# A three-part fp32 kernel: the first products of its recurrence into idle tiles, input loads moved, masks as steps of their own, and the state copied by DMA

## The chip, the cores and the metric

The kernel runs on one core of a Trainium2 chip. The metric is the device time of one execution in microseconds (us). A profile of one execution lists the instructions of each engine: PE (TensorE, matrix products; PEld is its weight load), DVE (VectorE), ACT (ScalarE), POOL (GpSimd) and SP (SyncE, which here only issues DMAs).

## What is computed

Batch 4, 8 heads, 768 time steps, head size 40, all fp32. First a recurrence on a 40 x 40 state for each batch and head, then a channel mix (a low-rank mix over time, two dense layers with relu), then an attention with 4 experts of which the 2 best are summed. Cut to what matters:

```python
for t in range(768):                      # the recurrence
    y[:, :, t] = einsum('bhd,bhde->bhe', r_t, state)
    Sa = einsum('bhde,bhe->bhd', state, a_t)
    state = state * w_t[:, :, None, :] - einsum('bhd,bhe->bhde', Sa, b_t) + einsum('bhd,bhe->bhde', v_t, k_t)
x = y.transpose(0, 2, 1, 3).reshape(4, 768, 320)
u = x + (x.T @ U @ V).T                   # the channel mix
x = u + relu(u @ w_ch1) @ w_ch2
# then causal softmax attention for each of 4 experts, weighted sum of the best 2
```

## The kernel before, in words

The recurrence is worked in chunks of 64 time steps: 12 chunks (`NC`) for 2 pairs of batches (`NBP`), 24 units (`NU`) in all. A unit holds 8 pairs of heads (`PP`). The change lies in `recurrence`; the channel mix and the attention behind it stay as they are.

For each unit there are three kinds of work:

- **Front.** `scaled(j)` makes running products of the decay on DVE (the scans of L195 and L203, tile `P`), scales two inputs into the tile `bkt` (L208) and a third in place (L216), and SP copies that one into the zeroed tile `ga` (L219). There are 16 sets (`NSET`) for 24 units: rows 40 to 63 and 104 to 127 of a set hold a third, "guest" unit's data, which `sent(j)` copies by DMA to the guest tiles `P_g` and `bkt_g` and to the guest's `ga` (L164). The sets are loaded into four slots at first (`ldt` twice and the unused part of `x` twice), later into two. `front(u)` then transposes on PE (L233, L243), and multiplies `bkt` with `ga` (L255); ACT copies this product `pg` from PSUM back over `bkt` (L258); POOL takes from it the diagonal blocks for the solve (`lx`, L263), masks it into `ga` (L266) and keeps a corner (`m21`, L270).
- **Solve.** For each group of 4 units `lanes(g)` inverts the triangular blocks on DVE: a transpose (L279), 30 steps of a product (L285) and a sum (L288), a transpose back into `tf` (L297). There are 6 groups.
- **Core and output.** `core(u)` needs `tf`, `ga`, `m21` and the state, works on PE and ACT in turns, and adds to the state `st` (L362, L364 on DVE; L367 puts it into the tile `uv` of the next unit). `outs(u)` transposes the tile `xu` (L381), which holds the unit's values and the state, multiplies (L403), masks (L396, DVE) and writes the unit's output (L416, L420, L426). The state gets into `xu` by `carry`: two POOL copies for each of 22 units (L306).

The order of all this is written out by hand in `ORDER_R`, a string with one letter for each step of a generator: `d` scaled, `g` sent, `f` fronts, `m` loads, `l` one step of a solve, `A` and `B` the cores of the two batch pairs, `p` and `q` their outputs, `z` the zeroing of tiles, `y` first loads, `u` the conversion of weights for the channel mix (L542 to L550), `x` a product for it. `WAIT` gives how many letters the masking, the output product and the state update are put off behind the PE work that they read. Each engine runs its instructions in the order in which the letters issue them, and SP issues its DMAs in that order too; each waits for what it reads and for the buffers that it writes.

The tiles `rbd` and `uvt` belong to the outputs and are not used before the first output.

Of the kernel before, what the change touches and what calls it, by code (L numbers as in the profile page):

```python
# [39 lines left out]

WAIT = (2, 3, 3)
ORDER_R = (
    'zddlllllldllllmgdlmgdlzfdldlglfmfgfzdgfdmfllyfgmlfffmfdfdfmmddllfflglmlgdffddgdglgllffldzl',
    'ffglldllllmlllfzylflllldflllflylfffldllflgldflflglffldlggylllfllgdmBffllAfflflflfffgAldlll',
    'BlmdlllfdfBgABAfqBAllfqlqBAddlgllldgmpdpldBlgllAqpgllfBAlffBAqfqqfpBAppflgllldddllffBmlffl',
    'qplfllqfqldpdlglflAlqffflBAgqplBdAgBlAfpqBpAplmlldldlfgdllgpqqBllllAflfglplAlBpfplAlBllAfl',
    'llfqBpfAmBqgqpdAlflldqlldlllllflffplqqgBlddfflllpplglfmlAdBggfdqllfpBABAflpllqBllplqlfddll',
    'glflqlfdfplBlfflmdpgqABfpfqlqldfABpABpplAllgfAqgBldqmAlfpdfdlplglffgBgllfplfddlfqllpffAfdl',  # L50
    'lgfqlqlAfllflllmlllBlAfABppABpgqfBqlqAddppfgllAllBlqdqllpdfggBlqlqldffAlBgAlBfpAqlpqBlffll',
    'ffflfllpflflfllpulpqAlBplAqlqBAllulqBllAlpqBpAxBlqlllxlllAlppqllxxlBAlllqulpBAqlqlBlABplpl',
    'AllppBxqllllqlllllAqlllpBplqqlABullplqBAllBAlpqplquBAllpqlpxxllluBApqpBlAqqlBAlluBAlqqppAq',
    'qpxlllullxxqppqllpqulplqlBplllxxllx',
)


def recurrence(ctx, tc, ld, vin, rv, ident, xs, keep, wpool, mix):
# [29 lines left out]
    tfs = [const.tile([128, 32, 32], F32, name=f"tf{i}") for i in range(2)]  # L88

    ldx = [x[:, NC // 3:].rearrange("p c f -> p (c f)")[:, :LDW] for x in xs]  # L90
    guests = [fpool.tile([128, PP, CW], F32, name="P_g"), fpool.tile([128, PP, 2, C], F32, name="bkt_g")]
    nc.gpsimd.memset(guests[0], 1.0)
    nc.gpsimd.memset(guests[1], 0.0)

    def slot(j):
        return (ldt + ldx)[j % 4 if j < 6 else j % 2]

    mix.spare = lambda: fpool.tile([128, 2 * (S // 4)], F32, tag="lx", name="spare")
    BK, GA, PC, LX, M21, TF, UP = {}, {}, {}, {}, {}, {}, {}

    def load_ld(j, a=0, b=LDW):
        nc.sync.dma_start(slot(j)[:, a:b], ld[j, :, a:b])

    def load_v(u):
        c, bp = divmod(u, NBP)
# [117 lines left out]
    def front(u):  # L223

        g, uu = divmod(u, GU)
        c, bp = divmod(u, NBP)
        P, early = PF[u], u < GU
        pc = PC[u] = const.tile([128, PP], F32, tag="pc", bufs=16, name=f"pc{u}")
        nc.scalar.activation(pc, P[:, :, C], AF.Copy)
        pt = ps.tile([128, 4, 2, D], F32, tag="f", bufs=3, name=f"pt{u}")  # L230
        for p in range(4):
            for b in range(2):
                nc.tensor.matmul(pt[64 * b:64 * b + 64, p], P[:, 2 * p + b, :C],  # L233
                                 ident.rearrange("p (r e) -> p r e", r=2)[:, :, :D], start=True, stop=True)
        nc.scalar.activation(xs[bp][:, c], pt.rearrange("p a r d -> p (a r d)"), AF.Copy)
        yield

        bkt = BKT[u]
        BK[u] = wpool.tile([128, PP, 2, D], F32, tag="bk", bufs=AHEAD + 4, name=f"bk{u}")
        for h in range(2):  # L240
            pb = ps.tile([128, HP, 128], F32, tag="f", bufs=3, name=f"pb{u}_{h}")
            for p in range(HP):
                nc.tensor.transpose(pb[:, p], bkt[:, h * HP + p].rearrange("p k t -> p (k t)"), ident)  # L243
            nc.scalar.activation(BK[u][:, h * HP:h * HP + HP],
                                                 pb.rearrange("p q (r e) -> p q r e", r=2)[:, :, :, :D], AF.Copy)
            yield

        ga = GA[u]
        m21 = M21[u] = const.tile([128, PP, 32], F32, tag="m21", bufs=AHEAD + 1, name=f"m21{u}")
        if uu == 0:  # L250
            LX[g] = fpool.tile([128, 32, 32], F32, tag="lx", name=f"lx{g}")
        for h in range(2):
            pg = ps.tile([128, HP, 2, C], F32, tag="o" if early else "f", bufs=3, name=f"pg{u}_{h}")
            for p in range(HP):
                nc.tensor.matmul(pg[:, p], bkt[:, h * HP + p].rearrange("p k t -> p (k t)"),  # L255
                                 ga[:, :, h * HP + p], start=True, stop=True)
            hs = slice(h * HP, h * HP + HP)
            nc.scalar.activation(bkt[:, hs], pg, AF.Copy)  # L258
            if h:
                for r in range(2):  # L260
                    for i in range(2):
                        q = slice(64 * r + 32 * i, 64 * r + 32 * i + 32)
                        nc.gpsimd.tensor_copy(LX[g][q, uu * PP:uu * PP + PP], bkt[q, :, r, 32 * i:32 * i + 32])  # L263
                for r in range(2):
                    z = slice(64 - 64 * r, 128 - 64 * r)
                    nc.gpsimd.affine_select(ga[z, r], bkt[z, :, r], [[0, PP], [1, C]], OP.is_gt, 0.0, base=0,  # L266
                                            channel_multiplier=-1)
                for r in range(2):
                    q = slice(64 * r, 64 * r + 32)
                    nc.gpsimd.tensor_copy(m21[q], bkt[q, :, r, 32:])  # L270
# [208 lines left out]
    for x in "".join(ORDER_R):
# [570 lines left out]
```

## Time and profile before

| | |
|---|---|
| median of 3 runs | 858.09 us (856.68 to 860.68) |
| the profiled execution | 858.54 us, of which the span of instructions is 856.8 |
| PE, DVE busy in the span | 780.3 us (91%), 579.5 us (68%) |
| ACT, POOL busy | 469.9 us (55%), 323.9 us (38%) |
| DMA packets, bytes | 53201, 61.47 MB |
| last solve ends (L297) | 324.0 us |

The span is counted from the first instruction. A busy share over the whole span is an average over stages with different limits, so the stages are looked at apart. A wait is put down to what came last. Durations on POOL are rough.

### The profile page before, as it was taken

What the parts mean: (1) busy time and instruction counts of PE and PEld (TensorE: products, weight loads), DVE (VectorE), ACT (ScalarE), POOL (GpSimd) and SP (SyncE); (2) the same over time, 40 slices, a digit from 0 to 9 for tenths busy, and PEclk for the clock granted to TensorE, in tenths of its full rate; (3) what the DMA queues carried; (4) which work ended last, traced back from release to release, by engine and by line L of the source; (5) the groups of instructions that cost most, each with busy time, mean ns of one, the idle gap of its engine ahead of it and who ended that gap; (6) DMA issues with size and microseconds to landing.
All of it is one profiled execution on the core that took longest, in us unless ns stands there. A gap on an engine that the chain in (4) does not pass through costs nothing.

```text
span 856.8 us, 22703 instructions
## 1 busy us (share of the span) xinstructions
PE 780.3 (91%) x9100; PEld 666.2 (78%) x9100; DVE 579.5 (68%) x1388; ACT 469.9 (55%) x1125; POOL 323.9 (38%) x456
## 2 busy tenths in 40 slices
PE   5666989989999897989899999999999999999997
PEld 4555888988898687877678888887778788887875
DVE  6599999988998997448624131322268868778773
ACT  3534867766677678723323231312168757767672
POOL 5664464536545324315513220202027344244430
PEclk9787999998999999899999999999999999999999
DMA  5554256555545364512100100000000010000101
GB/s 166 171 143 158 78 171 164 151 144 150 137 144 145 87 171 114 130 54 83 47 1 25 34 2 1 1 1 0 1 1 2 1 47 2 16 32 2 47 2 47
DMA packets 53201, 61.47 MB, mean 72 GB/s; under 512 B 31208, under 2 KB 38376, under 8 KB 51560
## 3 DMA queue, kind: packets, MB, share of 16 engines
q1 hardware_dynamic: 53096, 60.02, 24.6%
q8 instruction: 72, 1.18, 0.6%
q14 instruction: 33, 0.27, 0.1%
HBM read 47.46 MB, written 4.13 MB: 60 GB/s over the span
## 4 chain that ended last, share of the span: by engine, by line
PE 54%; DVE 19%; DMA 6%; issue 5%; ACT 4%; POOL 2%; SPq 1%; DVEq 0%; POOLq 0%; ACTq 0%
PE po L943 4%; PE ph L743 3%; PE pa L760 3%; PE ph L740 3%; PE pa L761 3%; PE pa L762 3%; PE ph L741 3%; PE ph L739 3%; PE tp L930 3%; DVE lt L288 3%; DVE tmp L285 3%; PE pn L403 2%; PE pw L343 2%; PE ps L890 2%; PE ps L889 2%
## 5 line engine op out<-in xcount | busy, mean ns | idle before, releaser
L913 POOL TENSOR_TENSOR P<-P,sm 128x128 f32<-128x128 f32 (+2 forms) x92 | 82.9, 931 | 127.6 <-DVE sm L903 115.4
L747 DVE SCALAR_TENSOR_TENSOR hl<-ph,hh 128x512 fp32r<-128x512 f32 x60 | 41.1, 690 | 118.6 <-ACT hh L746 116.1
L746 ACT ACTIVATE hh<-ph 128x512 fp32r<-128x512 f32 x60 | 35.1, 594 | 108.5 <-PE pa L762 101.2
L894 ACT ACTIVATE P<-ps,mx 128x640 f32<-128x640 f32 (+4 forms) x96 | 60.5, 634 | 26.1 <-DVE mx L892 18.1
L285 DVE TENSOR_TENSOR tmp<-lt 128x30 f32<-128x30 f32 (+9 forms) x180 | 70.3, 390 | 3.9
L288 DVE TENSOR_TENSOR lt<-lt,tmp 128x30 f32<-128x30 f32 (+9 forms) x180 | 69.0, 384 | 3.7
L892 DVE CUSTOM_DVE_ANT_0 ps<-ps,neg 128x640 f32<-128x640 f32 (+4 forms) x96 | 59.0, 639 | 7.6 <-PE ps L890 6.5
L263 POOL COPY lx<-bkt 32x256 f32<-32x256 f32 x64 | 30.0, 469 | 87.9 <-ACT bkt L258 85.8
L403 PE MATMUL pn<-rbd,uvt 128*128 128x128 f32 x384 | 54.9, 293 | 7.3 <-DMA uvt<-in_rin 5.7
L776 POOL TENSOR_TENSOR t<-t,ul 128x512 f32<-128x512 f32 x12 | 15.4, 1294 | 116.8 <-DVE t L775 116.7
L255 PE MATMUL pg<-ga,bkt 128*128 128x128 f32 x256 | 40.1, 318 | 19.6 <-DMA ga<-ldt 14.3
L403 PEld LDWEIGHTS pn<-rbd,uvt 128*128 128x128 f32 x384 | 49.6, 204 | 9.5 <-issue 4.9
L930 PE MATMUL tp<-ident,P 128*128 128x128 f32 x336 | 52.0, 276 | 1.8 <-ACT pt L934 0.8
L255 PEld LDWEIGHTS pg<-ga,bkt 128*128 128x128 f32 x256 | 36.6, 226 | 21.6 <-issue 12.7
L346 ACT ACTIVATE uv<-pw 32x320 f32<-32x320 f32 x96 | 41.1, 428 | 18.4 <-PE pw L343 16.7
L739 PE MATMUL ph<-uh,w 128*128 128x512 f32 x120 | 47.1, 399 | 1.7 <-ACT uh L728 1.6
L740 PE MATMUL ph<-ul,w 128*128 128x512 f32 x120 | 47.7, 397 | 0.6 <-DVE ul L729 0.6
L741 PE MATMUL ph<-uh,w 128*128 128x512 f32 x120 | 47.3, 396 | 0.0
L761 PE MATMUL pa<-hl,w 128*128 128x512 f32 x120 | 47.1, 392 | 0.0
L930 PEld LDWEIGHTS tp<-ident,P 128*128 128x128 f32 x336 | 39.4, 140 | 9.2 <-POOL P L913 2.7
L943 PE MATMUL po<-pt,vals 128*64 128x256 f32 (+3 forms) x320 | 45.1, 397 | 1.4 <-DVE o L959 1.0
L762 PE MATMUL pa<-hh,w 128*128 128x512 f32 x120 | 46.2, 391 | 0.0
(217 smaller groups left out, 2239.8 us busy)
## 6 DMA issues: line engine op xcount, KB each, us to landing
ldt<-in_ld SPq DMA_DIRECT2D x12, 1028.5 KB
uvt<-in_rin SPq DMA_DIRECT2D x48, 128.0 KB
rpt<-in_rin SPq DMA_DIRECT2D x24, 256.0 KB
rbd<-in_rin SPq DMA_DIRECT2D x48, 96.0 KB
uv<-in_vin SPq DMA_DIRECT2D x48, 80.0 KB
out<-o SPq DMA_DIRECT2D x24, 160.0 KB
ga<-ldt SPq DMA_DIRECT2D x28, 80.0 KB
room<-in_w SPq DMA_DIRECT2D x7, 320.0 KB
```

The costliest lines, as they stand in the source:

```text
L255: nc.tensor.matmul(pg[:, p], bkt[:, h * HP + p].rearrange("p k t -> p (k t)"), ga[:, :, h * HP + p], start=True, stop=True)
L285: nc.vector.tensor_tensor(tv, L[:, s + 1:, s:s + 1].to_broadcast([128, n, s]), L[:, s:s + 1, :s].to_broadcast([128, n, s]), op=OP.mult)
L288: nc.vector.tensor_tensor(L[:, s + 1:, :s], L[:, s + 1:, :s], tv, op=OP.add)
L403: nc.tensor.matmul(pn[h][:, p], ut[:, h * HP + p].rearrange("p r t -> p (r t)"), rbd[u % 2][:, :, h * HP + p], start=True, stop=True)
L739: nc.tensor.matmul(ph, w[:, 0, f], uh[:, ft], start=ft == 0, stop=False)
L740: nc.tensor.matmul(ph, w[:, 0, f], ul[:, ft], start=False, stop=False)
L741: nc.tensor.matmul(ph, w[:, 1, f], uh[:, ft], start=False, stop=False)
L761: nc.tensor.matmul(pa[ft], w[:, o:o + m], hl, start=False, stop=False)
L762: nc.tensor.matmul(pa[ft], w[:, 2 * DM - FT[2][0] + o:2 * DM - FT[2][0] + o + m], hh, start=False, stop=last)
L913: nc.gpsimd.tensor_tensor(p, p, sm[:, i:i + 1].to_broadcast([128, w]), op=OP.mult)
L930: nc.tensor.transpose(pt[:, j - j0], P[:, c:c + 128], ident)
L943: nc.tensor.matmul(po[64 * r:64 * r + 64, s0:w], VS[b][:, j, HD * e:HD * e + HD], PT[r][:, j, s0:], start=j == 0, stop=j == i1 - 1, skip_g ...
```

## The change

- The first four units' products `pg` are copied to `rbd` and `uvt` (the list `rooms`) instead of back over `bkt`; POOL reads them there.
- The masks (L266, L270) become a generator of their own, `kept(u)`, letter `k`, and can stand later than the copies for the solve.
- Set 1 is loaded complete in front of everything; set 2 is loaded by two DMAs that ACT issues; the loads from set 3 on are one DMA each, and the new order puts them ahead of DMAs of guests.
- `carry` copies the state into `xu` with two DMAs on SP instead of two POOL copies.
- `WAIT` and `ORDER_R` are new (the ten strings are not shown in full).

```diff
-WAIT = (2, 3, 3)
+WAIT = (1, 0, 2)
 ORDER_R = (
-    'zddlllllldllllmgdlmgdlzfdldlglfmfgfzdgfdmfllyfgmlfffmfdfdfmmddllfflglmlgdffddgdglgllffldzl',
+    'dddglzddlfzzfglgglldffldfdlmfddkfylgglldzdflmfldfdffffkdlgllllldfkfgdflmllfdflffdglgllzlfl',
...
+    rooms = [t.rearrange("p r q t -> p (r q t)").rearrange("p (q r t) -> p q r t", q=PP, r=2) for t in rbd] + uvt
...
-    def load_ld(j, a=0, b=LDW):
-        nc.sync.dma_start(slot(j)[:, a:b], ld[j, :, a:b])
+    def load_ld(j, a=0, b=LDW, queue=nc.sync):
+        queue.dma_start(slot(j)[:, a:b], ld[j, :, a:b])
...
     def loads():
-        for j in range(1, NSET):
-            for y in parts[j == 1:] if j < 4 else ((0, LDW),):
-                load_ld(j, *y)
-                yield
+        for j in range(3, NSET):
+            load_ld(j)
+            yield
...
-            nc.scalar.activation(bkt[:, hs], pg, AF.Copy)
+            gm = GM[u] = rooms[u] if early else bkt
+            nc.scalar.activation(gm[:, hs], pg, AF.Copy)
             if h:
                 for r in range(2):
                     for i in range(2):
...
-                        nc.gpsimd.tensor_copy(LX[g][q, uu * PP:uu * PP + PP], bkt[q, :, r, 32 * i:32 * i + 32])
-                for r in range(2):
-                    z = slice(64 - 64 * r, 128 - 64 * r)
-                    nc.gpsimd.affine_select(ga[z, r], bkt[z, :, r], [[0, PP], [1, C]], OP.is_gt, 0.0, base=0,
-                                            channel_multiplier=-1)
-                for r in range(2):
-                    q = slice(64 * r, 64 * r + 32)
-                    nc.gpsimd.tensor_copy(m21[q], bkt[q, :, r, 32:])
+                        nc.gpsimd.tensor_copy(LX[g][q, uu * PP:uu * PP + PP], gm[q, :, r, 32 * i:32 * i + 32])
...
+    def kept(u):
+        ga, gm = GA[u], GM[u]
+        m21 = M21[u] = const.tile([128, PP, 32], F32, tag="m21", bufs=AHEAD + 1, name=f"m21{u}")
+        for r in range(2):
+            z = slice(64 - 64 * r, 128 - 64 * r)
+            nc.gpsimd.affine_select(ga[z, r], gm[z, :, r], [[0, PP], [1, C]], OP.is_gt, 0.0, base=0,
+                                    channel_multiplier=-1)
+        for r in range(2):
+            q = slice(64 * r, 64 * r + 32)
+            nc.gpsimd.tensor_copy(m21[q], gm[q, :, r, 32:])
+        yield
...
     def carry(u):
-                nc.gpsimd.tensor_copy(xu[u % NBP][q, :, r, :D], st[u % NBP][q])
+                nc.sync.dma_start(xu[u % NBP][q, :, r, :D], st[u % NBP][q])
...
     parts = (n, LDW), (0, 2 * PP * C), (2 * PP * C, n)
-    for a, b in parts:
-        load_ld(0, a, b)
-    load_ld(1, *parts[0])
+    for j in range(2):
+        for a, b in parts:
+            load_ld(j, a, b)
...
+    for a, b in (parts[0], (0, n)):
+        load_ld(2, a, b, nc.scalar)
```

**SP at the start.** These are SP's issues before the change, from the 14th on (`x` holds the sets 2 and 3, `ldt` the sets 0, 1, 4, 5; set 2 is `x_66`, set 3 `x_67`):

```order
L102 DMA x_66<-in_ld 128x521
L164 DMA P_g<-P_149 24x520
L164 DMA P_g<-P_149 16x520
L219 DMA ga_128<-ldt_88 40x512 x2
L164 DMA bkt_g<-bkt_168 24x1024
L164 DMA bkt_g<-bkt_168 16x1024
L102 DMA x_66<-in_ld 128x1024
L107 DMA uv_98<-in_vin 64x320 x2
L164 DMA ga_126<-ldt_88 24x512
L164 DMA ga_126<-ldt_88 16x512
L102 DMA x_66<-in_ld 128x512
L102 DMA x_67<-in_ld 128x521
```

And these from the 14th on with the change:

```order
L165 DMA P_g<-P_149 24x520
L165 DMA P_g<-P_149 16x520
L219 DMA ga_130<-ldt_88 40x512 x2
L103 DMA x_67<-in_ld 128x2057
L108 DMA uv_98<-in_vin 64x320 x2
L165 DMA bkt_g<-bkt_196 24x1024
L165 DMA bkt_g<-bkt_196 16x1024
L165 DMA ga_128<-ldt_88 24x512
L165 DMA ga_128<-ldt_88 16x512
L219 DMA ga_253<-x_66 40x512 x2
L103 DMA ldt_87<-in_ld 128x2057
```

The loads of set 2 are gone from SP (ACT issues them in front of its first work), that of set 3 stands behind the second set's `ga`, and set 4 (`ldt_87`) follows after four pairs.

**POOL's work for the first solve.** Before, POOL's rows for the first four units were these, with the copies of the fourth unit (`bkt_294`) at the end:

```order
L263 COPY lx_189<-bkt_138 32x256 x4
L266 AFFINE_SELECT ga_124<-bkt_138 64x512 x2
L270 COPY m_188<-bkt_138 32x256 x2
L263 COPY lx_189<-bkt_168 32x256 x4
L266 AFFINE_SELECT ga_128<-bkt_168 64x512 x2
L270 COPY m_251<-bkt_168 32x256 x2
L263 COPY lx_189<-bkt_g 32x256 x4
L266 AFFINE_SELECT ga_126<-bkt_g 64x512 x2
L270 COPY m_314<-bkt_g 32x256 x2
L448 MEMSET sbd_104 128x640
```

With the change, from the first unit's masks on:

```order
L274 AFFINE_SELECT ga_126<-rbd_106 64x512 x2
L278 COPY m_229<-rbd_106 32x256 x2
L454 MEMSET sbd_104 128x640
L454 MEMSET sbd_105 128x640
L454 MEMSET st_112 128x320
L454 MEMSET st_113 128x320
L263 COPY lx_189<-rbd_107 32x256 x4
L274 AFFINE_SELECT ga_130<-rbd_107 64x512 x2
L278 COPY m_319<-rbd_107 32x256 x2
L263 COPY lx_189<-uvt_110 32x256 x4
L274 AFFINE_SELECT ga_128<-uvt_110 64x512 x2
L278 COPY m_343<-uvt_110 32x256 x2
```

After these come the fourth unit's copies from `uvt_111`, then two memsets of `rbd`, and only then the fourth unit's masks; the sources are `rbd` and `uvt` instead of `bkt`.

**SP behind the first solve.** With the change the state copies (L312, `xu<-st`) stand among the loads like this:

```order
L312 DMA xu_102<-st_112 40x8x40 x2
L103 DMA ldt_87<-in_ld 128x2057
L219 DMA ga_1240<-ldt_88 40x512 x2
L165 DMA bkt_g<-bkt_1156 24x1024
L165 DMA bkt_g<-bkt_1156 16x1024
L120 DMA uvt_111<-in_rin 64x8x64 x2
```

Before there was no such row on SP; the loads and guest copies behind it are now issued after it.

## Rows read from the trace of the kernel before

**Rows 1.** Stages: start:end, us, busy PE, PEld, DVE, ACT, POOL (instructions), PE clock, DMA share, GB/s.

```profile
0.00:43.60 43.60, 25.30 (x199) 22.92 (x200) 26.15 (x34) 18.41 (x35) 26.64 (x53) 0.89 0.55 168
77.80:324.00 246.20, 224.88 (x5132) 207.98 (x5132) 229.21 (x513) 178.06 (x450) 117.48 (x193) 0.97 0.50 140
324.00:370.40 46.40, 41.81 (x945) 37.27 (x946) 26.16 (x50) 32.03 (x79) 18.29 (x23) 0.93 0.44 110
```

**Rows 2.** Waits of DVE, 0 to 45: total us, times, longest.

```profile
DVE bkt L208 <- DMA x<-in_ld: 4.0, 1, 4.0
DVE P L195 <- DMA ldt<-in_ld: 3.7, 2, 3.1
```

**Rows 3.** Timeline of DVE, 0 to 90: start, duration, instruction, [idle before, releaser].

```profile
13.79 0.69 DVE L216 SCALAR_TENSOR_TENSOR ldt<-ldt,P 128x512 f32<-128x512 f32 x1 [0.79 <-DMA ldt<-in_ld]
...
17.24 1.31 DVE L195 TENSOR_TENSOR_SCAN P<-x,hot 128x520 f32<-128x520 f32 x1 [2.73 <-PE pt L233]
...
36.05 1.24 DVE L195 TENSOR_TENSOR_SCAN P<-ldt,hot 128x520 f32<-128x520 f32 x1 [3.07 <-DMA ldt<-in_ld]
...
41.57 1.97 DVE L279 STREAM_TRANSPOSE lt<-lx 128x1024 f32<-128x1024 f32 x1 [2.76 <-POOL lx L263]
...
43.77 1.23 DVE L208 TENSOR_TENSOR bkt<-ldt 128x1024 f32<-128x1024 f32 x1
...
75.83 1.97 DVE L297 STREAM_TRANSPOSE tf<-lt 128x1024 f32<-128x1024 f32 x1
```

**Rows 4.** Timeline of SP's issues, 0 to 100.

```profile
29.42 1.33 SPq L164 DMA_DIRECT2D P_g<-P  x2
30.80 0.58 SPq L102 DMA_DIRECT2D ldt<-in_ld  x1
```

**Rows 5.** Chain that ended last, 0 to 345: start, us, what.

```profile
140.49 5.83 DMA uvt<-in_rin
...
174.01 3.64 DMA ga<-ldt
...
338.34 4.13 DMA uvt<-in_rin
```

**Rows 6.** Timeline of POOL, 0 to 90.

```profile
16.64 2.55 POOL L263 COPY lx<-bkt 32x256 f32<-32x256 f32 x4 [9.17 <-ACT bkt L258]
...
22.26 1.70 POOL L263 COPY lx<-bkt 32x256 f32<-32x256 f32 x4
...
75.90 1.70 POOL L263 COPY lx<-bkt 32x256 f32<-32x256 f32 x4 [9.03 <-ACT bkt L258]
```

**Rows 7.** Groups, 66.5 to 77.8 (first row), else 77.8 to 324: busy, mean ns | idle.

```profile
L285 DVE TENSOR_TENSOR tmp<-lt 128x228 f32<-128x228 f32 (+11 forms) x12 | 3.8, 318 | 0.4
...
L285 DVE TENSOR_TENSOR tmp<-lt 128x228 f32<-128x228 f32 x10 | 4.5, 451 | 0.3
...
L285 DVE TENSOR_TENSOR tmp<-lt 128x30 f32<-128x30 f32 x10 | 2.5, 246 | 0.3
...
L285 DVE TENSOR_TENSOR tmp<-lt 128x30 f32<-128x30 f32 (+9 forms) x150 | 58.4, 390 | 3.0
L288 DVE TENSOR_TENSOR lt<-lt,tmp 128x30 f32<-128x30 f32 (+9 forms) x150 | 57.3, 382 | 2.9
...
L306 POOL COPY xu<-st 40x320 f32<-40x320 f32 x40 | 22.4, 561 | 48.3 <-PE pv L381 34.2 <-DVE st L364 12.5
```

**Rows 8.** Timelines of POOL and PE, 318 to 338.

```profile
322.13 0.94 POOL L306 COPY xu<-st 40x320 f32<-40x320 f32 x2 [2.21 <-PE pv L381]
...
334.23 1.53 PE L381 MATMUL pv<-ident,xu 128*128 128x128 f32 x12
```

**Rows 9.** DMA queues, 77.8 to 324: packets, MB, share of 16 engines.

```profile
q1 hardware_dynamic: 33559, 33.64, 49.0%
```

**Rows 10.** Timeline of DVE, 265 to 385: first and last of four steps of a weight conversion.

```profile
286.74 0.43 DVE L542 TENSOR_SCALAR ldt<-ldt 128x512 int32<-128x512 int32 x1
...
288.39 0.69 DVE L547 SCALAR_TENSOR_TENSOR ldt<-ldt 128x512 f32<-128x512 uint32 x1
```

More of the change, by code (lines that the diff above doesn't have):

```diff
@@ L37 @@
 NSET = 2 * NU // 3
-WAIT = (2, 3, 3)
+WAIT = (1, 0, 2)
 ORDER_R = (
-    'zddlllllldllllmgdlmgdlzfdldlglfmfgfzdgfdmfllyfgmlfffmfdfdfmmddllfflglmlgdffddgdglgllffldzl',
[L46 to L54, printed above, removed]
+    'dddglzddlfzzfglgglldffldfdlmfddkfylgglldzdflmfldfdffffkdlgllllldfkfgdflmllfdflffdglgllzlfl',
+    'lflgllgdlAldflylkfdfllllgffkflllllyfllllkfflfllgffgldggmfdfyBlfglfflffBdAflfBllAkdlklBflgl',
+    'lAlfmqBdAqlklflqlBgllAddBpdgdgfqBlpApmlfldflAfBqlgqAkplqfllpflAlpBpllllfgdldlfqlqflgAmBlfl',
+    'llfllfllllplplqddflABdplkkAlgBqBllAqllfBqfAgpdpgfpllpldBAdfplflqqlklplAmllglllBflAlBfqllgm',
+    'fBldflfApBqfgAlqklllplffdlfdlflqlpBAdkgdlfglqfdfpqplgddBmAflfAqpllBAlfqlBglkqlAppBpffdfpgl',
+    'ldfldAflmBlqflpqkdflAdlBqpfdfBllklABAgpplfgfgBdfdqpflffAlqlgllglllqllllBllfflqlfllmgppfqAm',
+    'fqlflBdAfpfgAdBAkdBkqflfqlABlqppApplllkAdBdglpglfdqfdqgpdlfqfAlBfllpgllllAlBfllflgllqfflBp',
+    'fkplffAqlBlqffqBlllllAqlllklplpABllqllpllABlABlqllApppllpBllllqllAqqBlqlllAlplBllBlkllllll',
+    'upBpAuqBApxlxllxAxpqpBxlAqllulAqqlqlABpplllABpplplulllBqqpAxBlqqxulAlBlqlpqABlulqqplBllABl',
+    'AlpBqpqlqqpllxxppuqpqAlpqlupqxxulllxllllx',
 )
@@ L98, in recurrence @@
     mix.spare = lambda: fpool.tile([128, 2 * (S // 4)], F32, tag="lx", name="spare")
-    BK, GA, PC, LX, M21, TF, UP = {}, {}, {}, {}, {}, {}, {}
-    def load_ld(j, a=0, b=LDW):
-        nc.sync.dma_start(slot(j)[:, a:b], ld[j, :, a:b])
+    BK, GA, GM, PC, LX, M21, TF, UP = {}, {}, {}, {}, {}, {}, {}, {}
+    def load_ld(j, a=0, b=LDW, queue=nc.sync):
+        queue.dma_start(slot(j)[:, a:b], ld[j, :, a:b])
     def load_v(u):
@@ L248, in front @@
         ga = GA[u]
-        m21 = M21[u] = const.tile([128, PP, 32], F32, tag="m21", bufs=AHEAD + 1, name=f"m21{u}")
         if uu == 0:
@@ L475, in recurrence @@
             "d": chain(*[scaled(j) for j in range(NSET)]),
-            "g": chain(*[sent(j) for j in range(NSET)]), "m": loads(), "y": firsts(), "f": fronts(), "z": ready(), "l": more(),
+            "g": chain(*[sent(j) for j in range(NSET)]), "m": loads(), "y": firsts(), "f": fronts(),
+            "k": chain(*[kept(u) for u in range(NU)]), "z": ready(), "l": more(),
             "u": mix.weights(mix.sources()[0], ldt, (guests[0].rearrange("p q t -> p (q t)"), hot)),
```

## The prediction

> **What bounds the kernel now.** I read the table of stages first, then the waits of VectorE (DVE), then three timelines. The stage table [rows 1] cuts the profiled execution at the ends of the first and the last triangular solve of the recurrence (77.8 and 324 us), at the start of the first (43.6) and where the channel mix begins (370.4). The stage from 77.8 to 324 is bound by DVE: 229.2 us busy of 246.2, the rest being mostly gaps of some 0.02 us between instructions; TensorE (PE) follows with 224.9. Before that it is different: from 0 to 43.6 DVE works only 26.2 us. So the start holds the one large idle piece of the busiest engine. Its waits there [rows 2] are for input loads, 4.0 and 3.7 us. The DVE timeline [rows 3] shows where they lie and two more: the third set's scan starts at 17.24 (the view names PE, but that set's load, issued at 13.9, landed just then), the fifth's at 36.05, the first solve's transpose at 41.57 after 2.76 us of waiting for GpSimd (POOL). From there to the end of the solve's last transpose at 77.80 no wait is left.
>
> **The change part by part.**
>
> *Loads.* ACT issues the third set at the start (two DMAs), the second set is complete before any guest DMA, the fourth is one DMA. By hand, with the durations of before: the last step of DVE's second set started at 13.79 after a wait of 0.79 for its load; without it the set ends at 13.7. The third set's scan then starts at 13.9 instead of 17.24, and the rest of the set (5.1 us of work) follows without the 4.0 for its product: it ends at 19.2. SP issues the fourth set's load behind the pair `ga<-ldt` of the second, at 15.2 to 15.8. A load of this size takes from its issue at 30.80 to the scan at 36.05, so 5.25 us [rows 3, 4]; the fourth set can start at 21 and ends at 26.1. The fifth set's load stands behind four pairs of about 1.35 us [rows 4], issued at 21.2, there at 26.5: its scan starts 9.5 us early. Its product must wait until the buffer it writes is copied to the guest tile: that pair goes out at 27.6, behind the fourth set's `ga`, and such a copy inside SBUF landed 3.64 us after issue [rows 5], so at 31.2; DVE is through at 32.6.
>
> *Idle tiles and masks as own steps.* The first four products go to `rbd` and `uvt`, so ACT need not wait for the guest copies out of `bkt`, and `bkt` need not wait for POOL's masks. The solve needs POOL's four groups of copies. POOL's first group, copies and masks, took 5.6 us from 16.64 to the next at 22.26, with 2.55 for its copies where the next needed 1.70 [rows 6]. Three groups of 4 to 5.6, some 2 us of memsets between, and the fourth unit's copies of 1.7 to 2.55, from 16.6 on, end between 32.3 and 38; the fourth unit's masks and two more memsets now stand behind these copies. I take 34.5, nearer the short end, since only the first group was the long one. The stretch from 41.57 to 77.80 was 36.2 us and loses the product now done ahead (1.23), so the first solve ends at 69.5 instead of 77.8: **-8.3 us**, with -4 (POOL interfered with, a late load) and -10 as ends.
>
> *POOL's state copies.* The view of waits has no row for interference between engines, but durations show it: the last twelve products of the first solve, for most of which POOL stood idle (9.03 us before 75.90 [rows 6]), took 318 ns on average; in the stage from 77.8 to 324 the same twelve shapes averaged 368 (means of the twelve forms add to 4.42 us, first and last shown) [rows 7]. That is 14% of 58.4 + 57.3 us, 15.8 us. The state copies are 22.4 us of POOL's 117.5 there [rows 1, 7], 19%; with them **-3.0 us** go. Below: 0, if only the larger POOL instructions interfere. Above: each copy holds DVE for its whole length whenever DVE is in such a product (115.7 of 246.2 us, 47%): -10.5 us. I take the share, as it is nearest to what the rows show on average. The Trainium skill, page "SBUF — State Buffer", section "Who interferes with whom", says that a VectorE instruction with two SBUF inputs and a GpSimd instruction that reads SBUF exclude each other for the whole instruction; the slower shapes here agree in direction. By that rule the gain would lie towards the upper end, the rival "whole lock" below.
>
> *The copies as DMAs.* 44 more issues on SP, 40 of them before 324, at 0.58 us each [rows 4]. The transfer itself is not in the trace. Its nearest row is `uvt<-in_rin`, 512 runs of 256 B, which landed 4.13 and 5.83 us after issue [rows 5]; a state copy has 320 runs of 160 B. So 5.3 to 7.0 us in place of POOL's 0.95 for the pair. What covers this: the copy at 322.13 was done at 323.07, and the transposes that read it started at 334.23, 11 us later [rows 8]. So I cost the transfer at 0; without the cover it would be up to 6 us at each of 11 steps of the recurrence. Traffic: 33,559 packets took 49.0% of 16 engines in the stage [rows 9], 57 ns each; 40 x 320 more add 12,800, so 46 us of the 16 engines or 19 points of share, to 68%. No row shows a limit there, so 0, and up to +6 for later landings. The Trainium skill, page "DMA: Bandwidth & Descriptors", section "Specifications", speaks against this part: runs under 512 B don't reach line rate. It gives no price, and no run here shows one for runs of 160 B.
>
> *Order behind the first solve.* The counts of DVE instructions between solves are the same (10 sets, 36 masks, 20 state updates), except that one weight conversion (2.34 us for its first four steps [rows 10] and a fifth) and one output product stand behind the last solve instead of before it: -3.5. In the tail four groups of transposes (0.51 each [rows 8]) and half a unit's output come in front of PE, which is busy 41.8 of 46.4 us [rows 1]: +2.8, and the conversion falls into idle time of DVE (20 us). I take 0, +3 and -3 as ends. The shorter delays (WAIT) move DVE's masks and PE's order by a step or less; no row prices it, and I put it at 0 within the same ends.
>
> **Sum.** The profiled execution took 858.54 us (span 856.8), 0.45 above the median of 858.09. 858.5 - 8.3 - 3.0 = **847.2**, forecast 847. All but the tail lies in the recurrence; the channel mix and the attention are only shifted.
>
> **Rivals.**
> 1. *SP becomes the limit (slower).* A state copy on SP waits for DVE's update and for PE's transposes of the old state, and nothing behind it is issued. On POOL these waits were 48.3 us in the stage [rows 7]. SP issues 239 transfers there (by its timeline); at 0.58 that is 139 us of 246, so 107 are free, and 48.3 + 23.2 would take 71 of them. Behind the copies stand `P_g`, `ga` and set loads. For: the chain of waits ran through such a load on SP (5.83). Against: these loads are emitted ahead of their use. If half of the 48.3 us cannot be covered, DVE runs dry for 24 us: 847 + 24 = **871**. It decides when a copy waits longer than the lead of the load behind it.
> 2. *The start is won and lost again.* If PE, busy 91% of the stage, or a later load sets the pace from 77.8 to 324, only a few of the 8.3 us arrive, and the copies' gain does not: **855 to 858**. For: PE's share [rows 1]. Against: DVE's share is higher still, 93%, and what it lacks is nearly all gaps between instructions.
> 3. *Whole lock.* The copies hold DVE in full: 858.5 - 8.3 - 10.5 = **840**. For: the rule named above. Against: the average over all POOL work is far lower.
> 4. *The early loads do not land early*, because the third set from ACT shares the 16 engines with the first two: the fourth set then still lands at 24 or later, and the start gives 4: **851**.
>
> **How the numbers follow.** Forecast 0.50, rival 1 0.12, rival 2 0.18, rival 3 0.10, rival 4 0.10. About 0.5% (4.3 us) is what a measurement can tell from no change. Faster by more: forecast, rivals 3 and 4, less their upper edge: 0.69. Within: most of rival 2 and that edge: 0.18. Slower: rival 1 and a mishap with the shared issue queue: 0.13. The range takes in rivals 2 to 4 and the ends of the unknown costs that lie between them (start -10, order -3 and a part of the lock below; start -4, landing +6 above), and leaves out rival 1 and what lies under the whole lock: 838 to 859.
>
> **What would show it.** Right: the load waits of [rows 2] under 4 us together; the first transpose near 34.5 and the first solve's end near 69.5; the DVE products of the stage nearer 318 than 368 ns for the same shapes; the last solve ending 9 to 14 us earlier than 324; state DMAs landing in 3 to 6 us with nobody waiting for `xu`. Wrong: the first solve not before 75; PE waiting for `xu`; waits of DVE for loads (`ldt`, `ga`, `uvt`) that grow by over 10 us between the solves.

## The result and the profile after

The changed kernel takes 866.40 us (median of 20 runs, 860.85 to 877.27), the kernel before 857.49 beside it (20 runs, 851.67 to 863.23). The ratio is 1.0106, 95% interval 1.0082 to 1.0130: slower by 1.1%. The forecast was 847.0, the range 838 to 859, so both are missed, and on the wrong side. The profiled execution of the changed kernel took 861.91 us (span 860.2), one of its fastest, while that of before was near its median; so only the runs give the size of the loss, and the trace tells where the forecast gains went.

The stages of the changed kernel, cut nearly as in [rows 1] (columns as there; the first row ends inside the first transpose, at 41.1, where that of before ends behind it):

```profile
0.00:41.10 41.10, 25.94 (x234) 23.78 (x235) 26.61 (x34) 18.91 (x36) 28.20 (x51) 0.92 0.64 207
75.80:323.80 248.00, 222.17 (x5109) 204.83 (x5108) 219.93 (x506) 175.59 (x445) 93.13 (x159) 0.97 0.53 137
323.80:374.00 50.20, 44.40 (x988) 39.27 (x988) 32.65 (x54) 35.04 (x87) 14.78 (x15) 0.97 0.65 163
```

Between the first and the last solve DVE works 9.3 us less than before and PE 2.7 less, yet the stage is 1.8 us longer. The first solve ends at 75.8 instead of 77.8 and the last one at 323.7 instead of 324.0: the 2 us of the start and DVE's 9.3 are both lost on the way. The tail behind the last solve is 3.8 us longer.

**The start.** DVE's timeline, the rows that answer to [rows 3]:

```profile
14.66 1.24 DVE L195 TENSOR_TENSOR_SCAN P<-x,hot 128x520 f32<-128x520 f32 x1 [0.19 <-issue]
...
23.10 1.24 DVE L195 TENSOR_TENSOR_SCAN P<-x,hot 128x520 f32<-128x520 f32 x1 [3.30 <-DMA x<-in_ld]
...
32.22 1.47 DVE L195 TENSOR_TENSOR_SCAN P<-ldt,hot 128x520 f32<-128x520 f32 x1 [4.21 <-PE pt L233]
...
40.08 1.98 DVE L285 STREAM_TRANSPOSE lt<-lx 128x1024 f32<-128x1024 f32 x1 [3.06 <-POOL lx L263]
...
73.83 1.94 DVE L303 STREAM_TRANSPOSE tf<-lt 128x1024 f32<-128x1024 f32 x1
```

The third set starts as forecast (14.66, forecast 13.9), the fourth 2 us late, and the first transpose stands at 40.08 instead of 34.5. What it waits for is told by three more timelines, SP's, PE's and POOL's:

```profile
17.23 0.48 SPq L103 DMA_DIRECT2D x<-in_ld  x1
...
19.09 1.40 SPq L165 DMA_DIRECT2D bkt_g<-bkt  x2
```

```profile
25.72 1.94 PE L243 MATMUL pb<-ident,bkt_g 128*128 128x128 f32 x8 [4.06 <-DMA bkt_g<-bkt]
```

```profile
17.51 2.97 POOL L263 COPY lx<-rbd 32x256 f32<-32x256 f32 x4 [10.04 <-ACT rbd L258]
...
24.62 4.06 POOL L263 COPY lx<-rbd 32x256 f32<-32x256 f32 x4
...
31.77 2.55 POOL L263 COPY lx<-uvt 32x256 f32<-32x256 f32 x4 [0.85 <-ACT uvt L258]
34.39 3.14 POOL L274 TENSOR_SCALAR_AFFINE_SELECT ga<-uvt 64x512 f32<-64x512 f32 x2
...
38.34 1.70 POOL L263 COPY lx<-uvt 32x256 f32<-32x256 f32 x4
```

The load of set 3 stands ahead of the guest copy `bkt_g` now; the copy, issued at 19.09, is there only at 25.7, and the guest is the third of the four units. Behind it POOL masks the third unit (from 34.39) before it copies the fourth (38.34), whose product was in place at 35.6. But POOL waits for the guest only 0.85 us, in front of 31.77. From 17.51 to 40.04 that is all its idle time, so POOL's own work sets the first transpose.

**Between the solves.** The waits of DVE, 75.8 to 323.8, and DVE's products and sums, 79 to 322 (columns as in [rows 7]):

```profile
DVE P L195 <- DMA ldt<-in_ld: 4.1, 3, 3.3
DVE P L195 <- issue: 3.6, 2, 3.4
DVE lt L285 <- POOL lx L263: 3.1, 3, 1.5
DVE ldt L551 <- DMA ldt<-in_v: 3.0, 1, 3.0
```

```profile
L291 DVE TENSOR_TENSOR tmp<-lt 128x30 f32<-128x30 f32 (+9 forms) x150 | 55.9, 373 | 2.8
L294 DVE TENSOR_TENSOR lt<-lt,tmp 128x30 f32<-128x30 f32 (+9 forms) x150 | 54.9, 366 | 3.1
```

The products went from 390 to 373 ns and the sums from 382 to 366 [rows 7]: 33 ns x 150 = 5.0 us less, more than the 3.0 forecast. In e1 below, which differs from the changed kernel in the state copies alone, they are (77 to 326)

```profile
L294 DVE TENSOR_TENSOR lt<-lt,tmp 128x30 f32<-128x30 f32 (+9 forms) x150 | 59.7, 398 | 3.1
L291 DVE TENSOR_TENSOR tmp<-lt 128x30 f32<-128x30 f32 (+9 forms) x150 | 57.9, 386 | 2.8
```

so by this pair it is 6.8 us. Against it, the rows of waits for a DMA, those of PE and DVE between 78 and 324 added up, went from 6.3 to 16.6 us (DVE's alone from 4.1 to 7.6). PE's and the issues of the state copies on SP (op, count: shortest/median/longest ns):

```profile
PE pg L254 <- DMA ga<-ldt: 4.1, 3, 1.5
PE pn L409 <- DMA uvt<-in_rin: 3.2, 2, 2.5
```

```profile
L312 SPq DMA_DIRECT2D xu<-st x44: 767/834/1732, 89.7 to 350.6; - x44
```

Each takes 0.83 us of SP, not the 0.58 of a set's load [rows 4]. The guest copies of the kernel before took 0.66 to 0.72 already (medians of L164), so SP had less free time than the 107 us of the prediction.

### The profile page after: what moved, and what is told of

Same layout as the page of the kernel before. It is cut to its first block, busy times and chain, and to the rows that moved or that the text cites. A ratio compares the mean times of both kernels' runs of the same rounds, so it can differ in the third digit from the quotient of the medians.

```text
span 860.2 us, 22675 instructions
## 1 busy us (share of the span) xinstructions
PE 776.6 (90%) x9100; PEld 662.5 (77%) x9100; DVE 579.0 (67%) x1388; ACT 469.7 (55%) x1125; POOL 299.0 (35%) x412
## 3 DMA queue, kind: packets, MB, share of 16 engines
q1 hardware_dynamic: 66896, 61.22, 26.4%
## 4 chain that ended last, share of the span: by engine, by line
PE 43%; DVE 8%; ACT 4%; issue 3%; DMA 3%; POOL 1%; SPq 0%; DVEq 0%; POOLq 0%; ACTq 0%
PE po L952 4%; PE ph L752 3%; PE pa L769 3%; PE pa L770 3%; PE pa L771 3%; PE ph L749 3%; PE tp L939 3%; PE ph L750 3%; PE ph L748 3%; PE ps L899 2%; PE ps L898 2%; PE pa L766 1%; PE pa L765 1%; DVE ps L901 1%; ACT P L903 1%
## 5 line engine op out<-in xcount | busy, mean ns | idle before, releaser
L756 DVE SCALAR_TENSOR_TENSOR hl<-ph,hh 128x512 fp32r<-128x512 f32 x60 | 41.1, 690 | 117.3 <-ACT hh L755 114.8
L291 DVE TENSOR_TENSOR tmp<-lt 128x30 f32<-128x30 f32 (+9 forms) x180 | 67.9, 377 | 3.7
L294 DVE TENSOR_TENSOR lt<-lt,tmp 128x30 f32<-128x30 f32 (+9 forms) x180 | 66.9, 372 | 4.0
L263 POOL COPY lx<-bkt 32x256 f32<-32x256 f32 x52 | 25.0, 481 | 107.0 <-ACT bkt L258 81.5
L409 PE MATMUL pn<-rbd,uvt 128*128 128x128 f32 x384 | 51.8, 284 | 9.0 <-DMA uvt<-in_rin 3.2
L409 PEld LDWEIGHTS pn<-rbd,uvt 128*128 128x128 f32 x384 | 46.5, 194 | 11.2 <-ACT w L328 2.5
L254 PE MATMUL pg<-ga,bkt 128*128 128x128 f32 x256 | 36.3, 298 | 13.7 <-DMA ga<-ldt 13.1
L254 PEld LDWEIGHTS pg<-ga,bkt 128*128 128x128 f32 x256 | 33.4, 209 | 15.5 <-issue 11.9
```

What stands on the lines that cost most here:

```text
L291: nc.vector.tensor_tensor(tv, L[:, s + 1:, s:s + 1].to_broadcast([128, n, s]), L[:, s:s + 1, :s].to_broadcast([128, n, s]), op=OP.mult)
L409: nc.tensor.matmul(pn[h][:, p], ut[:, h * HP + p].rearrange("p r t -> p (r t)"), rbd[u % 2][:, :, h * HP + p], start=True, stop=True)
```

## The experiments

All ratios are against the kernel before, run on the same chip in the same rounds. 1% is 8.6 us.

**State copies: which part of the change loses the time (e1, e2).** e1 undoes them in the changed kernel, e2 does them alone in the kernel before:

```diff
-                nc.sync.dma_start(xu[u % NBP][q, :, r, :D], st[u % NBP][q])
+                nc.gpsimd.tensor_copy(xu[u % NBP][q, :, r, :D], st[u % NBP][q])
```

> The changed kernel with the state copies back on POOL (nothing else undone). Theory O (the new order behind the first solve, with its shorter delays, costs the time; the state copies by DMA do not): still slower than before, by 0.5 to 1.5% (862 to 870 us), since the order is kept and POOL's interference with DVE's products comes back. Theory C (the state copies as DMAs cost it: they wait at the head of SP's queue and the loads behind them come late): the loss goes, 850 to 857 us, ratio 0.99 to 1.00 against before.

> The kernel before with only the state copies changed to two DMAs on SP. Theory O: no loss, ratio 0.994 to 1.002 (852 to 859 us), the products of DVE between the solves a little shorter than 390 ns. Theory C: slower by 0.6% or more (863 us up), waits of DVE and PE for loads longer.

e1: 859.66 us, 1.0014 (0.9982 to 1.0047). e2: 867.09 us, 1.0127 (1.0080 to 1.0174). Theory O falls in both: without the DMAs the change costs nothing that can be measured, and the DMAs alone cost as much as the whole change or more (the intervals overlap). From e1 to the changed kernel it is 1.0106/1.0014 = 1.0092, 7.9 us. In e2's trace, an execution at its median, SP and DVE show one place where it happens:

```profile
279.71 1.75 SPq L313 DMA_DIRECT2D xu<-st  x2
281.51 1.36 SPq L610 DMA_DIRECT2D ldt<-in_u  x2
282.91 2.00 SPq L610 DMA_DIRECT2D ldt<-in_v  x4
```

```profile
286.49 0.36 DVE L550 TENSOR_SCALAR ldt<-ldt 128x384 int32<-128x384 int32 x1 [8.58 <-DMA ldt<-in_v]
...
288.94 1.95 DVE L286 STREAM_TRANSPOSE lt<-lx 128x1024 f32<-128x1024 f32 x1
```

The same in the kernel before:

```profile
269.81 1.29 SPq L602 DMA_DIRECT2D ldt<-in_u  x2
271.14 2.01 SPq L602 DMA_DIRECT2D ldt<-in_v  x4
```

```profile
276.53 0.36 DVE L542 TENSOR_SCALAR ldt<-ldt 128x384 int32<-128x384 int32 x1 [2.62 <-DMA ldt<-in_v]
...
279.72 1.98 DVE L279 STREAM_TRANSPOSE lt<-lx 128x1024 f32<-128x1024 f32 x1
```

The weight loads stand behind a state copy that SP could issue only at 279.71, after 3.6 us without an issue; PE's transposes of the old state end at that time. The loads go out 11.7 us later than before, DVE waits 8.58 us for them instead of 2.62, and the sixth solve starts 9.2 us later and ends 8.6 later (332.6 for 324.0). The fifth had ended 4.0 later. SP has no free time in this place: in the kernel before it issues from 262.1 to 273.6 with gaps of 0.1 us at most.

**Start and order (e3, e4).** With the copies on POOL, the change's start is followed by the old order, or the old start by the change's order. There is no diff to show: the strings are cut at the first solve's end and joined. In e4 only the letters are the old ones: sets 1 and 2 are loaded in front of everything as with the change, set 2 by ACT.

> The start of the changed kernel (loads, idle tiles, masks as own steps, the changed order up to the first solve's end), then the order and the delays of before, state copies on POOL. Both theories: the first solve ends about 2 us earlier than before (75.8 instead of 77.8), as in the changed kernel. Theory O: these 2 us arrive at the end, ratio 0.996 to 0.999, and no loss is left. Theory C says the same; a rival to both, that the start itself disturbs what follows, gives 1.003 or more.

> The start of before (its loads and order up to the first solve's end; masks as own steps directly behind the products; idle tiles in use), then the order and the shorter delays of the change, state copies on POOL. Theory O: the whole loss, and the 2 us of the start on top: ratio 1.008 to 1.015 (865 to 871 us). Theory C: no loss, 0.998 to 1.003.

e3: 856.80 us, 1.0005 (0.9982 to 1.0028), though its first solve ends at 74.5 (77.8 before). e4: 866.29 us, 1.0111 (1.0080 to 1.0142), inside theory O's range. But its second solve alone takes from 76.0 to 128.7, 6 us longer than e1's (77.9 to 124.4), so the seam may be what costs; e1, with the same order behind the start that belongs to it, is the better test. e4's start is no worse than the change's, though the load of set 3 stands behind the guest copies in it: the first transpose is at 38.05 (39.22 in e1, 40.08 in the changed kernel), the first solve ends at 74.2 (74.9, 75.8).

**Another queue for the copies (e5, e11).** `nc.gpsimd.dma_start` and `nc.scalar.dma_start` in `carry`, else the changed kernel.

> The changed kernel with the state copies as the same 44 DMAs, issued by POOL instead of SP. Theory H (head of the queue: on SP a copy that waits for the state's transposes or update holds back the loads behind it): as good as with the copies done by POOL itself, 856 to 862 us, ratio 0.998 to 1.005. Rival T (the transfers themselves: 14,080 more packets of 160 bytes, or their late landing): as slow as the changed kernel, 864 us up, ratio 1.007 or more.

> The changed kernel with the state copies as DMAs issued by ACT, directly behind ACT's own copies of the transposed state or of the updated state, so that ACT has waited for nearly the same already. Theory H: the loss goes, 855 to 862 us, ratio 0.998 to 1.005. Rival T: no better than the changed kernel, 864 us up. A rival that gives 862 to 866 us: ACT, 176 us busy of 248 between the solves, pays the issues (44 at about 0.8 us).

e5: 869.42 us, 1.0150 (1.0098 to 1.0202). e11: 866.39 us, 1.0109 (1.0063 to 1.0154). Theory H's forecast fails in both: with SP rid of the copies the loss stays. This alone does not clear SP's queue, since each run may put a new cost in place of the old: in e5 POOL waits 32.4 us for PE's transposes in front of these issues, and e11 lies just beyond the rival that ACT pays for them. e9 below is the cleaner test. e5's rows of the line tell what POOL pays, and, as no other queue does, the time to landing:

```profile
L312 POOL DMA_DIRECT2D xu<-st x44: 712/715/892, 89.1 to 355.0; - x44
...
DMA to landing us min/median/max: 2.3/4.1/7.5
```

An issue costs POOL 0.715 us; a copy by POOL itself took 0.561 [rows 7]. On ACT it is 0.80.

**Waits, packets or number (e9, e10, e13, e14).** In the kernel before: e9 splits each state copy, the first pair of heads by SP, seven by POOL; the other three add DMAs to POOL's copies that wait for no engine's result.

```diff
-                nc.gpsimd.tensor_copy(xu[u % NBP][q, :, r, :D], st[u % NBP][q])
+                nc.sync.dma_start(xu[u % NBP][q, 0, r, :D], st[u % NBP][q, 0])
+                nc.gpsimd.tensor_copy(xu[u % NBP][q, 1:, r, :D], st[u % NBP][q, 1:])
```

```diff
                 nc.gpsimd.tensor_copy(xu[u % NBP][q, :, r, :D], st[u % NBP][q])
+                m = M21[max(M21) - 1 - len(CARRIED) % 3].rearrange("p q t -> p (q t)")[:, :250].rearrange("p (n t) -> p n t", t=25)
+                z = slice(64 * r + 32, 64 * r + 64)
+                nc.sync.dma_start(m[z, :, :24], ident[z, None, :24].to_broadcast([32, 10, 24]))
```

The second diff is e10; e13 cuts its DMA to one partition and one run, e14 writes 20 runs of 11 elements instead of 10 of 24.

> The kernel before with an eighth of each state copy (the first of the 8 pairs of heads) as a DMA on SP, seven eighths still by POOL. SP issues the same 44 DMAs at the same places with the same waits as in e2, but they move 1,760 packets instead of 14,080. Theory H (a copy at the head of SP's queue waits for the state's transposes or its update, and the loads behind it come late): the loss of e2, ratio 1.008 or more. Rival T (the packets): at most 1.003. Rival N (the number of DMAs alone, by their issue on SP and the eight semaphores that they share in turn): the loss of e2 here and in e10 too.

> The kernel before, state copies on POOL, and at each of them two more DMAs on SP with 320 packets each of 96 bytes, from the identity into a part of the tiles m21 that nothing reads: 14,080 packets and 44 issues that wait for no result of another engine. Theory H: no loss, ratio 0.997 to 1.003. Rival T: 1.007 or more. Rival N: 1.007 or more.

> The kernel of e10 with each of its 44 added DMAs cut to one packet of 96 bytes. Theory N (each DMA costs by its issue on SP and by taking one of the eight semaphores that all DMAs share in turn, whatever it moves): the loss of e10 stays, ratio 1.004 to 1.008. Theory T (the 14,080 packets cost): it goes, 0.998 to 1.002.

> The kernel of e10 with twice the packets in the same 44 DMAs (28,160 packets of 44 bytes). Theory T: twice the loss, 1.012 to 1.016. Theory N: the loss of e10, 1.005 to 1.009.

| | packets in each of 44 DMAs | waits for the state | ratio (95%) |
|---|---|---|---|
| e9 | 40 | yes | 1.0042 (1.0007 to 1.0077) |
| e13 | 1 | no | 1.0062 (1.0026 to 1.0099) |
| e10 | 320 | no | 1.0071 (1.0038 to 1.0104) |
| e14 | 640 | no | 1.0086 (1.0056 to 1.0117) |

Theory T alone falls with e13, and e13 and e14 lie where theory N has them: 44 DMAs of one packet that wait for nothing cost 0.62%, 5.3 us, and what more packets add (0.24% from 1 to 640) is within the intervals. e9 fits none of the three as they were put: it has SP's waits and the number of e2 and loses a third of e2's 1.27%. So neither the number nor the waits, at 40 packets a DMA, make up e2's loss. In e10's trace the weight loads of e2's one place go out between the times of before and of e2:

```profile
276.75 1.34 SPq L605 DMA_DIRECT2D ldt<-in_u  x2
278.13 2.83 SPq L605 DMA_DIRECT2D ldt<-in_v  x4
```

They are 6.9 us later than before (3.3 of it had come by the fifth solve's end) though no added DMA waits for a result; e2's wait for the transposes comes on top. An issue of one packet is no shorter than one of 320 (e13, then e10):

```profile
L309 SPq DMA_DIRECT2D m<-ident x44: 699/748/1744, 80.8 to 344.3; - x44
```

```profile
L309 SPq DMA_DIRECT2D m<-ident x44: 591/652/1617, 81.0 to 350.9; - x44
```

44 x 0.75 = 33 us more of issues on SP, most of them between the solves. Which half of N it is (the issue, or the eight semaphores that SP's DMAs use in turn in the traces) was not tried; SP's rows of waits on a DMA don't grow (78 to 324, added up: 16.1 us before, 13.5 in e13, 13.9 in the changed kernel), so what the traces show is the issue.

**What a microsecond is worth between the solves (e7, e8, e15).** In the kernel before; e7 and e8 leave work out, e15 adds some to the start:

```diff
+            if g == 0 or s not in (14, 15, 16, 17):
...
-            if c > 0:
+            if c < 0:
...
-        nc.vector.transpose(L, LX[g].rearrange("p x t -> p t x"))
+        for _ in range(1 if g else 5):
+            nc.vector.transpose(L, LX[g].rearrange("p x t -> p t x"))
```

> The kernel before with the steps 14 to 17 of the solves two to six left out (40 of 300 products and sums, 19.5 us of DVE by their rows; that part of the inverse is not computed). Theory V (DVE sets the pace between the first and the last solve): the time falls by 17 to 20 us, ratio 0.977 to 0.981. Rival I (PE, and waits for one another in fixed orders, set it as much): by 3 to 10 us, 0.988 to 0.997.

> The kernel before with the products of the state in the outputs (L416) left out: 16 instructions in each of 22 units, about 0.76 us of PE in each by their timeline, 12 us between the solves and 3 to 4 in the tail; that term of the output is not computed. Theory V: only the tail's 3 to 4 us are won, ratio 0.995 to 0.997. Rival I: 8 to 15 us, 0.982 to 0.991.

> The kernel before with the transpose ahead of the first solve done five times (four more of 1.97 us on DVE, so the first solve ends 7.9 us later, at 85.7). Theory S (the first solve's end counts in full): 7 to 8.5 us slower, ratio 1.008 to 1.010. Rival L (between the solves the start's time is lost or made up): 0 to 4 us, 1.000 to 1.005.

e7: 851.78 us, 0.9929 (0.9901 to 0.9958). e8: 852.82 us, 0.9930 (0.9897 to 0.9962). e15: 863.75 us, 1.0043 (1.0013 to 1.0072). Theory V falls with e7: of 19.5 us taken from DVE 6.1 arrive (3.6 to 8.5 by the interval). Of some 15 taken from PE, 3 to 4 of them in the tail, 6.0 arrive; e8 lies between the two theories and its interval touches both. And of the 8.7 us by which e15's first solve ends later (86.5) 3.7 arrive, as rival L has it. The stage of e7, 77.8 to 321.8, in an execution of 857.12 us, its slowest:

```profile
77.80:321.80 244.00, 224.82 (x5132) 208.64 (x5132) 208.56 (x474) 179.66 (x451) 117.12 (x193) 0.96 0.51 141
```

DVE is down from 229.2 to 208.6 us and the stage from 246.2 to 244.0. Neither engine alone sets the pace. That they wait for one another, with orders fixed on every engine, is the likely reading; it was not traced further.

**A better start (e6, e12, e16).** e6 is e3 with two moves in the order string, e12 loads set 3 from ACT too, e16 puts e6's moves into e1:

```diff
-...ffldfdlmfddkfylgglldzdflmfldfd...dfkfgdflmllfdflffdg...
+...ffldfdlfddkflgglldzdmyflmfldfd...dffgdflmllfdflfkfdg...
```

> The kernel of e3 (new start, order and delays of before behind it, state copies on POOL) with two things moved in the start: the guest copies bkt_g and ga of the first pair of sets stand in front of the load of set 3, and the masks of the third unit behind the fourth unit's copies for the solve. By the rows of the changed kernel the third unit's product, which waited for the guest copy until 25.7, starts some 4 us earlier; the first transpose comes at 32 to 36 instead of 39.1, the first solve ends at 66 to 70. Theory S (an earlier start counts in full once it is larger): 851 to 854 us, ratio 0.992 to 0.996. Rival L (what the start wins is lost again before the third solve, because fronts and loads there are no earlier): 855 to 859 us, 0.997 to 1.002.

> The kernel of e6 with the load of set 3 issued by ACT behind that of set 2, so that the fourth scan needs not wait until 27.5. In the trace: that scan near 20 instead of 27.5, the first transpose at 33 to 36 instead of 39.0, the first solve's end at 66 to 69. Theory S (the start counts in full): 850 to 853 us, ratio 0.990 to 0.994. Rival L (a start that is earlier is lost between the solves, where PE and DVE wait for one another): 855 to 858, 0.996 to 1.000.

> The changed kernel with state copies on POOL (e1) and the two moves of e6 in its start: a try for a kernel that beats both. If the start of e6 and the new order add up: the first solve 1 to 2 us earlier than in e1, 853 to 857 us, ratio 0.994 to 0.999; if the start does not count: 1.000 to 1.003, as e1.

e6: 856.85 us, 0.9974 (0.9942 to 1.0006). e12: 855.88 us, 1.0002 (0.9965 to 1.0039). e16: 857.14 us, 0.9982 (0.9953 to 1.0012). None differs from before by more than its interval. e6's trace shows the guest in time and the gain spent elsewhere (PE, DVE, POOL):

```profile
23.07 1.95 PE L254 MATMUL pg<-ga,bkt_g 128*128 128x128 f32 x16
```

```profile
27.50 1.61 DVE L195 TENSOR_TENSOR_SCAN P<-x,hot 128x520 f32<-128x520 f32 x1 [7.87 <-DMA x<-in_ld]
...
39.01 1.93 DVE L285 STREAM_TRANSPOSE lt<-lx 128x1024 f32<-128x1024 f32 x1
```

```profile
29.80 7.40 POOL L263 COPY lx<-uvt 32x256 f32<-32x256 f32 x8
```

The third unit's product starts at 23.07 instead of 27.45, but now the load of set 3 is late, DVE's fourth set starts at 27.50, and the transpose, which stands behind the sets on DVE, is where it was in e3 (39.12). POOL does not wait for the guest any more, but its copies still end at 37.2 only: the last eight took 7.40 us. e12 missed its signs too: the fourth scan starts at 22.37, but the second set waits 2.54 us for its load, DVE waits 4.84 us for POOL, and the first transpose stands at 40.52 (33 to 36 expected).

**The state copied by ACT (e17, e18).** No DMA, and nothing on POOL:

```diff
-                nc.gpsimd.tensor_copy(xu[u % NBP][q, :, r, :D], st[u % NBP][q])
+                nc.scalar.activation(xu[u % NBP][q, :, r, :D], st[u % NBP][q], AF.Copy)
```

> The kernel before with the state copies done by ACT (44 copies of about 0.43 us, directly behind ACT's copies of the transposed or updated state) instead of POOL: no DMA is added, and POOL's copies still go from beside DVE's products. If what was hoped of the change (POOL's copies gone) is worth the 3.0 us forecast: 853 to 856 us, ratio 0.994 to 0.998. By e7, where 19.5 us less of DVE gave 6 to 7, DVE's 4 to 5 us are worth 1 to 2: 0.998 to 1.000. Rival A (ACT's 19 us more cost as much as DVE wins): 1.000 to 1.006.

> The kernel of e6 with the state copies done by ACT: the best start and no DMA for the state, a try for a kernel that beats both. If the two add up: 0.993 to 0.997 of before (851 to 855 us); by rival A: 0.998 to 1.004.

e17, the kernel before with this line alone: 851.28 us, 0.9945 (0.9912 to 0.9979), faster than both kernels. e18: 857.19 us, 1.0017 (0.9986 to 1.0048): e6's start and ACT's copies don't add up, and on top of that start the ACT copies gain nothing (e6 alone 0.9974). e17's copies, and its products and sums, 79 to 318:

```profile
L306 ACT ACTIVATE xu<-st x44: 466/470/474, 92.4 to 337.9; 40x320 f32<-40x320 f32 x44
```

```profile
L285 DVE TENSOR_TENSOR tmp<-lt 128x30 f32<-128x30 f32 (+9 forms) x150 | 56.7, 378 | 3.0
L288 DVE TENSOR_TENSOR lt<-lt,tmp 128x30 f32<-128x30 f32 (+9 forms) x150 | 56.1, 374 | 2.9
```

12 + 8 ns off 150 of each is 3.0 us of DVE; the 4.7 us gained are more than that, and by e7's price 3.0 us of DVE are worth 1. So POOL's 48.3 us of waits in front of these copies [rows 7], with its copies for the solve queued behind, are a likely part, which was not tried by itself.

## Why the prediction was wrong

**The premise.** "The stage from 77.8 to 324 is bound by DVE" was read from its busy share, 93%. e7 shows that a microsecond of DVE is worth about 0.3 there; e8 gives 0.4 for PE, the tail included. A share of 93% beside one of 91% does not tell which engine binds, and here neither did alone.

**The loads and the first solve, -8.3 us.** This step failed twice. Its size: the first solve ends 2.0 us earlier, not 8.3. The term that was mis-sized is POOL's work. Three groups of copies and masks were taken at 13 to 14 us together, "since only the first group was the long one"; they took 18.0 (5.2, 6.3 and 6.5), and the first began 0.9 late. Already before the change they took 15.6 (5.6, 4.8 and 5.2), the third with the longest copies of all:

```profile
30.69 2.97 POOL L263 COPY lx<-bkt_g 32x256 f32<-32x256 f32 x4 [3.62 <-ACT bkt_g L258]
```

The third unit's masks, 4.0 us, still stood ahead of the fourth's copies. The hand timing also gave the guest copies no later landing behind a load of 1 MB, but of that only POOL's 0.85 us of waiting reaches the transpose. And the step's worth: e3, 3.3 us earlier, gives 1.0005, and e15, 8.7 us later, gives 3.7 us. This is rival 2, a start won and lost again (855 to 858): e3 and e6 took 856.8 and 856.9. Rival 4 named a late load of set 3; it came at 23.1, where 24 was the mark.

**POOL's copies gone, -3.0 us.** DVE's products and sums lost 3.0 us in e17, 5.0 from the kernel before to the changed one and 6.8 from e1 to it, so the forecast is the low end. Its worth was not seen: at e7's price 3.0 to 6.8 us of DVE are 1 to 2 at the end, so e17's 4.7 must come in the main from something else, which is not shown. The Trainium skill's rule that the two engines exclude each other for a whole instruction ("SBUF — State Buffer", "Who interferes with whom") gave up to 10.5; the rows agree in direction and show a third to two thirds of that.

**The copies as DMAs, 0.** This term lost the case. "What covers this" looked at the reader of the copy, 11 us later, and rightly: no row of the changed kernel has PE waiting for `xu<-st`. The cost lies on the issuing side. From e1 to the changed kernel the exchange costs 7.9 us; with the 4.7 that e17 finds in POOL's copies gone, the DMAs themselves would cost some 12 to 13, an estimate that takes the two to add up. Of this e13 accounts for 5.3 by the number of DMAs alone. Rival 1 (871) had the sign and the place, and its counter-argument, "107 are free", was the error: free time on an in-order queue, summed over a stage, is no slack where the issues stand close and what stands behind them is needed soon, as at e2's weight loads. But its mechanism, a copy that waits at the head of SP's queue, is only a part: e2's trace has it at 279.71, yet e9 has those waits too and loses 3.6. What makes up the rest of e2's loss, beyond number, waits and packets taken one at a time, stays open. The 19 points of DMA share did not come: queue q1 moved from 49.0 [rows 9] to 51.5%, with some 4,000 other packets gone from the stage; over the whole run it went from 24.6 to 26.4%:

```profile
q1 hardware_dynamic: 42349, 33.12, 51.5%
```

The Trainium skill ("DMA: Bandwidth & Descriptors", "Specifications") wants 512 bytes for line rate. No run here shows that rate, and what e13, e10 and e14 lose is not in the runs: one packet in each DMA loses as much, within the intervals, as 320 or 640.

**Order, 0.** The sum was right: e1 has 1.0014 with the new order, delays and start. That its two halves cancel was not what happened. The tail pays: from the last solve's end to the mix's first transposes (L720, with the change L729) it is 45.8 us before, 48.0 in e1 and 50.4 with the change, one execution each, so some 2.2 by the order (+2.8 forecast) and as much again with the state DMAs. The -3.5 of DVE's work put behind the last solve does not show: in e1 that solve ends at 325.4, with the change at 323.7, before at 324.0.

Of the marks of wrong, one came: the first solve ended after 75. DVE's waits for loads between the solves grew by 3.5 us, with PE's by 10.3, where over 10 of DVE's alone was the mark. PE never waits for the copies of `xu`. Of the marks of right none came whole: the load waits of the start are 4.8 us and not under 4, the first transpose is 5.6 late, the products of the twelve shapes average 355 ns, nearer 368 than 318, the last solve ends 0.3 earlier, and the landing of the copies is seen in e5 alone (2.3 to 7.5 us).

## What to carry to other kernels

A DMA in place of a small copy cost an issue of 0.65 to 0.83 us on an in-order queue here, however little it moved; look at what stands behind the issues before moving work to "free" time there. Another engine may be worth a try: ACT gained 0.55% with the same copies in e17, though nothing on top of another start (e18). Before pricing a saving on the busiest engine, look at the second busiest: where both are over 90%, a microsecond of either was worth 0.3 to 0.4 here. A chain worked out by hand needs every group's own duration: POOL's second and third were in the trace. And an earlier start is worth what the next stages can use of it: make it later once, which is easy, and see how much arrives.

## What the runs showed of the hardware

- A DMA of one packet took SP 0.75 us to issue (median), one of 320 packets 0.65, a state copy of 320 runs 0.83 on SP, 0.80 on ACT, 0.715 on POOL.
- Small packets are cheap for the DMA engines: in e11 ACT's queue went from 288 packets and 0.3% to 14,808 and 1.9% of 16 engines over 865.6 us, so about 15 ns each by estimate; the 57 ns of the forecast, an average over larger packets, was four times that.
- POOL's copies suffer beside DVE as DVE does beside POOL: in the start of the changed kernel four copies for the solve took 1.70 us while DVE stood idle (38.34) and 4.06 beside DVE's scan and products of the fourth set (24.62). Which of the two suffers varies: at 44.23 four copies took 1.70 again, and it was the solve's 84-element product and sum beside them that took 0.45 and 0.40 us, where they took 0.24 and 0.25 at 71.56 with POOL idle.
